# Attention with a compressive memory in front of a gated layer: the memory term as 64 more keys of the half score blocks

## The chip, the core and the metric

The kernel runs on one core of one Trainium2 chip. The metric is device time in microseconds, the median of several runs; the time before is 565.52 us.

## What is computed

A batch of 4 with 8 heads, 576 positions and a head width of 64, all in float32. Each head adds two things, weighted with a gate g per head: causal softmax attention, and a retrieval from a memory matrix M with a normaliser z.

```python
scores = scale * np.matmul(q, k.transpose(0, 1, 3, 2))
scores = np.where(causal, -1000000000.0, scores)
scores = scores - scores.max(-1, keepdims=True)
a = np.exp(scores)
a /= a.sum(-1, keepdims=True) + 1e-09
local = np.matmul(a, v)
def phi(x):
    return np.where(x > 0, x, np.exp(x) - 1.0) + 1.0
q_p = phi(q)
mem_ret = np.einsum('bhsd,bhde->bhse', q_p, M_prev)
mem_norm = np.einsum('bhsd,bhd->bhs', q_p, z_prev)[..., None] + 1e-06
g = 1.0 / (1.0 + np.exp(-beta))[None, :, None, None]
out = g * (mem_ret / mem_norm) + (1 - g) * local
```

The 2304 positions x 512 columns of `out` then go through a gated layer: `((x @ w1) * (x @ w2)) @ w3 @ w_out`, 512 to 1024 to 1024 to 512.

## The kernel before

**Pairs.** The work goes by pairs of heads: 16 of them, 0 to 15, four to a batch. A pair's q and k lie transposed in one tile `raw`, head a of the two in partitions 64a to 64a + 63. Queries are cut into a first chunk of 64 and four of 128 (chunks c = 0 to 4); chunk c sees KE[c] = 64, 192, 320, 448, 576 keys. So a chunk has c full key blocks of 128 and one half block of 64.

**A pair on the engines.** TensorE makes the scores of both heads (s_all, L205; chunk 0 of both heads in one product with the block-diagonal tile `qd`, s_mm0, L191). VectorE reduces them with the mask into the tiles sm (s_red, L182). ScalarE takes the exponential (s_exp, L215). VectorE normalises (s_norm, L224; the sums also carry 1 - g). TensorE transposes each 128x128 block (t_mm, L234, and L255 for chunk 0), with the half blocks filled up by 64 columns of zeros, and ScalarE copies the blocks into `pt` (L265). Then TensorE multiplies `pt` with the values v, head by head into two halves of the columns of one bank pair x (pv_mm, L281). `fin` splits x into a high and a low part, `xs` (L292 on ScalarE, L293 on VectorE).

**The memory term** comes from q in its untransposed layout, `qn`. mem_a: ScalarE, the negative part's exponential (L138, L139). mem_b: VectorE adds (L144), GpSimd multiplies with z (L146). mem_c: VectorE sums (L151), and three small operations make g over the norm (L152, L153, L157); GpSimd multiplies the features with it (L159). mem_t: TensorE transposes the features in five blocks (L165), ScalarE copies them to `mt` (L167). mem_mm: TensorE multiplies `mt` with a block-diagonal tile of the memory matrices, `md` (L271, L272), into the same x that pv_mm then adds to.

**The gated layer** runs between these steps as fill. In batch 0 the fill is w3 @ w_out (L427), with the unpacking of all weights (ScalarE L314, VectorE L318, L319; for the gate weights also L326, L327). From batch 1 on it is the gated layer of the batch before: gemm1 (L477, 12 products per half, evicted by ScalarE L483 and VectorE L486, split by ScalarE L488 and GpSimd L489) and gemm2 (L497, copied out by VectorE L502). A table, ORDER, gives the order of steps in a pair; each F in it is a slot of fill, 13 per pair. The framework's scheduler then sets the final order on each engine: it puts steps earlier or later by its own priorities where data allow.

**Loads** all go through SyncE's queue, in order: raw (L109), chunk 0's q into `qd` (L113), v (L119), qn (L124), z (L127), per batch the memory matrices (L133), the weights (L303, L388). An issue waits there until its target is free.

Of the kernel before, what the change touches and what calls it, by code (L numbers as in the profile page):

```python
# [8 lines left out]
F32 = mybir.dt.float32  # L9
# [4 lines left out]
ALU = mybir.AluOpType  # L14
# [7 lines left out]
    "lv mt t1 c c F "  # L22
# [3 lines left out]
    "t4b t5 F "  # L26
    "mm pv ma F "
    "fin F "
    "F "
    "ss mb F "  # L30
# [12 lines left out]
def attention_moe_kernel(  # L43
# [22 lines left out]
    PT = 1920  # L66
# [10 lines left out]
    z_p = pool("z")  # L77
# [16 lines left out]
    sm = [[None] + [const.tile([128, KE[c] + 64], F32, name=f"sm{a}{c}") for c in range(1, 5)] for a in range(2)]  # L94
    qd = const.tile([128, 128], F32, name="qd")
    md = const.tile([128, NC, 128], F32, name="md")
# [4 lines left out]
    raw_t, v_t, qn_t, z_t, mt_t, pt_t, sums_t, stat = ({} for _ in range(8))  # L101
# [4 lines left out]
    def load_qk(p):  # L106
        b, h = heads(p)
        t = raw_t[p] = qk_p.tile([128, 2, S], F32, tag="raw", name="raw")
        nc.sync.dma_start(out=t, in_=qkt[b, h:h + 2].rearrange("h d t s -> (h d) t s"))  # L109
        if p == 0:  # L110
            load_raw(1)
        for a in range(2):
            nc.sync.dma_start(out=qd[64 * a:64 * a + 64, 64 * a:64 * a + 64], in_=qkt[b, h + a][:, 0, 0:64])  # L113

    def load_v(p):
        b, h = heads(p)
        t = v_t[p] = v_p.tile([128, 2, 5, D], F32, tag="v", name="v")
        for a in range(2):
            nc.sync.dma_start(out=t[:, a], in_=v[b, h + a])  # L119

    def load_qn(p):
        b, h = heads(p)
        t = mem_p.tile([128, 5, 2, D], F32, tag="qn", name="qn")
        nc.sync.dma_start(out=t, in_=qn[b, h // 2])  # L124
        zt = z_p.tile([128, 2, D], F32, tag="z", name="z")
        zs = z_prev[b, h:h + 2]
        nc.sync.dma_start(out=zt, in_=bass.AP(tensor=zs.tensor, offset=zs.offset, ap=[[0, 128], [D, 2], [1, D]]))  # L127
        qn_t[p], z_t[p] = t, zt

    def load_m(b):  # L130
        src = m_prev[b].rearrange("d (j t) e -> d t j e", t=2)
        for a in range(2):
            nc.sync.dma_start(out=md[64 * a:64 * a + 64, :, 64 * a:64 * a + 64], in_=src[:, a])  # L133
# [14 lines left out]
    def mem_c(p):  # L148
        t, e = qn_t[p], stat.pop(("e", p))
        n = st_p.tile([128, 10, 1], F32, tag="n", name="n")  # L150
        nc.vector.tensor_reduce(out=n, in_=e.rearrange("p t h d -> p (t h) d"), axis=AX.X, op=ALU.add)  # L151
        nc.vector.tensor_scalar(out=n, in0=n, scalar1=1e-6, scalar2=None, op0=ALU.add)  # L152
        nc.vector.reciprocal(out=n, in_=n)  # L153
        h0 = 2 * p % H
        n3 = n.rearrange("p (t h) o -> p t (h o)", h=2)
        gb = g_sb[:, h0:h0 + 2].rearrange("p (o h) -> p o h", o=1).to_broadcast([128, 5, 2])
        nc.vector.tensor_tensor(out=n3, in0=n3, in1=gb, op=ALU.mult)  # L157
        tv = t.rearrange("p t h d -> p (t h) d")
        nc.gpsimd.tensor_tensor(out=tv, in0=tv, in1=n.to_broadcast([128, 10, D]), op=ALU.mult)  # L159

    def mem_t(p):
        t = qn_t.pop(p)
        x = ps_x.tile([128, 1024], F32, tag="x", name="x")
        for i in range(5):
            nc.tensor.transpose(x[:, 384 + 128 * i:512 + 128 * i], t[:, i].rearrange("p h d -> p (h d)"), ident)  # L165
        mt = mt_t[p] = mem_p.tile([128, S], F32, tag="mt", name="mt")
        nc.scalar.activation(out=mt, in_=x[:, 384:960], func=ACTF.Copy)  # L167
# [63 lines left out]
    def t_mm(p, what):  # L231
# [3 lines left out]
        if what in ("4a", "4b", "3a", "3b"):  # L235
            c, a = int(what[0]), "ab".index(what[1])
            for kc in range(4):
                tr(128 * kc, c, a, kc)
            s = 128 if c == 4 else 0
            d = pt[:, a, s:s + 1792].rearrange("p (k q) -> p k q", q=448)[:, :, 320:448]  # L240
            jobs = [(ps.rearrange("p (k q) -> p k q", q=128), d)]
        elif what in ("2", "1"):
            c = int(what)
            for a in range(2):
                for kc in range(2):
                    tr(256 * a + 128 * kc, c, a, kc)
            q = 128 * c - 64
            jobs = [(
                ps.rearrange("p (a k q) -> p a k q", a=2, q=128),
                pt[:, :, 0:896].rearrange("p a (k q) -> p a k q", q=448)[:, :, :, q:q + 128],  # L250
            )]
        elif what == "h":
            for a in range(2):
                tr(128 * a, 2, a, 2)
            nc.tensor.transpose(ps[:, 256:384], sm0, ident)  # L255
            jobs = [
                (ps[:, 0:256].rearrange("p (a q) -> p a q", a=2)[:, :, 64:128], pt[:, :, 1152:1216]),
                (ps[:, 256:384].rearrange("p (a q) -> p a q", a=2), pt[:, :, 0:64]),
            ]
        else:  # L260
            for a in range(2):
                tr(128 * a, 4, a, 4)
            jobs = [(ps[:, 0:256].rearrange("p (a q) -> p a q", a=2)[:, :, 64:128], pt[:, :, 1024:1088])]
        for s, d in jobs:
            nc.scalar.activation(out=d, in_=s, func=ACTF.Copy)  # L265

    def mem_mm(p):
        x = stat["x", p] = ps_x.tile([128, 1024], F32, tag="x", name="x")
        mt = mt_t.pop(p)
        lhsT = md[:, p % NC]  # L270
        nc.tensor.matmul(x[:, 384:512], lhsT=lhsT, rhs=mt[:, 0:128], start=True, stop=False)  # L271
        nc.tensor.matmul(x[:, 512:960], lhsT=lhsT, rhs=mt[:, 128:576], start=True, stop=False)  # L272

    def pv_mm(p):
        x, pt, vv = stat["x", p], pt_t.pop(p), v_t.pop(p)
        for kc in range(5):
            off = 1024 if kc == 4 else 576 * kc
            for q0, q1 in ((0, 128), (128, 576)) if kc == 0 else ((128 * kc, 576),):
                for a in range(2):
                    o = off + q0 - 128 * kc  # L280
                    nc.tensor.matmul(  # L281
                        x[64 * a:64 * a + 64, 384 + q0:384 + q1], lhsT=vv[:, a, kc], rhs=pt[:, a, o:o + q1 - q0],
                        start=False, stop=(q0 == 0 or kc == 4),
                    )
# [3 lines left out]
    def fin(p):  # L288
        x = stat.pop(("x", p))[:, 384:960]
# [257 lines left out]
    def pair_step(p, F):  # L547
        nx = p + 1 < NP
        ops = dict(
            mt=(1, lambda: mem_t(p)),  # L550
# [9 lines left out]
            t5=(1, lambda: t_mm(p, "5")),  # L560
# [11 lines left out]
            mm=(1, lambda: mem_mm(p)),  # L572
# [3 lines left out]
            mb=(nx, lambda: mem_b(p + 1)),  # L576
            mc=(nx, lambda: mem_c(p + 1)),
# [21 lines left out]
    nc.gpsimd.memset(md, 0.0)  # L599
    for a in range(2):  # L600
        nc.vector.memset(qd[64 * a:64 * a + 64, 64 - 64 * a:128 - 64 * a], 0.0)
    for c in range(1, 5):
        for a in range(2):
            nc.vector.memset(sm[a][c][:, KE[c]:KE[c] + 64], 0.0)
    nc.vector.memset(sm0[:, 64:128], 0.0)
# [5 lines left out]
    s_all(0)  # L611
    s_mm0(0)
# [37 lines left out]
    for b in range(B):  # L650
        load_m(b)
# [41 lines left out]
```

## Time and profile before

| | |
|---|---|
| median of 3 runs | 565.52 us (565.14 to 566.21) |
| profiled execution, first to last instruction | 564.3 us |
| TensorE busy | 542.7 us, 96% |
| VectorE busy | 281.2 us, 50% |
| ScalarE busy | 276.7 us, 49% |
| GpSimd busy | 106.7 us, 19% |

The profile is of one execution of its own, and of its time only the span is given; the median of the runs stands 1.2 us above it. Busy shares are averages over the whole span: batch 0, with the weights' unpacking, has other limits than what follows.

### The profile page before, as it was taken

What the parts mean: (1) busy time and instruction counts of PE and PEld (TensorE: products, weight loads), DVE (VectorE), ACT (ScalarE), POOL (GpSimd) and SP (SyncE); (2) the same over time, 40 slices, a digit from 0 to 9 for tenths busy, and PEclk for the clock granted to TensorE, in tenths of its full rate; (3) what the DMA queues carried; (4) which work ended last, traced back from release to release, by engine and by line L of the source; (5) the groups of instructions that cost most, each with busy time, mean ns of one, the idle gap of its engine ahead of it and who ended that gap; (6) DMA issues with size and microseconds to landing.
All of it is one profiled execution on the core that took longest, in us unless ns stands there. A gap on an engine that the chain in (4) does not pass through costs nothing.

```text
span 564.3 us, 9257 instructions
## 1 busy us (share of the span) xinstructions
PE 542.7 (96%) x3440; PEld 433.6 (77%) x3440; DVE 281.2 (50%) x896; ACT 276.7 (49%) x723; POOL 106.7 (19%) x137
## 2 busy tenths in 40 slices
PE   4899989799999999999999999999999999999997
PEld 2344544458896979787978898798969797998995
DVE  6986899759653436263626272624534351111110
ACT  5656775749562637173725464354625361220210
POOL 1101202010430122212230313031301220220210
PEclk9899999999999999999999999999999999999999
DMA  7991646612111202121213021311112000000001
GB/s 294 417 375 51 218 132 224 208 49 94 40 62 44 87 28 69 57 88 30 67 29 106 28 55 35 100 48 39 58 43 88 23 2 20 20 1 37 1 1 56
DMA packets 23068, 48.31 MB, mean 86 GB/s; under 512 B 6896, under 2 KB 13040, under 8 KB 21488
## 3 DMA queue, kind: packets, MB, share of 16 engines
q1 hardware_dynamic: 23024, 47.72, 25.1%
q8 instruction: 27, 0.44, 0.3%
q14 instruction: 17, 0.14, 0.1%
HBM read 43.00 MB, written 4.72 MB: 85 GB/s over the span
## 4 chain that ended last, share of the span: by engine, by line
PE 83%; DVE 8%; ACT 4%; DMA 3%; issue 1%; SPq 0%; POOL 0%; DVEq 0%; ACTq 0%; POOLq 0%
PE m L477 37%; PE m L497 18%; PE s L234 8%; PE x L281 7%; PE s L205 5%; PE m L427 3%; DMA wst<-w 2%; PE x L272 2%; PE sx L205 2%; PE x L165 1%; ACT sm L215 1%; DMA wst<-w_out 1%; DVE sm L224 1%; DVE wsp L327 1%; ACT pt L265 1%; DVE w3s L319 1%
## 5 line engine op out<-in xcount | busy, mean ns | idle before, releaser
L477 PE MATMUL m<-xs,wsp 128*128 128x288 f32 x1536 | 223.5, 299 | 0.0
L477 PEld LDWEIGHTS m<-xs,wsp 128*128 128x128 f32 x1536 | 206.9, 188 | 1.2
L489 POOL TENSOR_TENSOR ht<-a,ht 128x288 fp32r<-128x288 f32 (+2 forms) x96 | 59.0, 628 | 261.6 <-ACT ht L488 242.3
L215 ACT ACTIVATE sm<-sm,mx 128x320 f32<-128x320 f32 (+3 forms) x144 | 82.6, 575 | 45.2 <-DVE mx L182 45.1
L497 PE MATMUL m<-wH,ht 128*128 128x512 f32 x288 | 95.4, 398 | 0.0
L265 ACT ACTIVATE pt<-s 128x512 f32<-128x512 f32 (+1 forms) x144 | 63.8, 497 | 27.7 <-PE s L234 27.4
L486 DVE SCALAR_TENSOR_TENSOR a<-m,a 128x288 f32<-128x288 f32 x64 | 29.2, 456 | 91.7 <-PE m L477 87.4
L427 PE MATMUL m<-wo,w3s 128*128 128x512 f32 x128 | 63.5, 625 | 5.7 <-DVE w3s L319 3.8
L234 PE MATMUL s<-ident,sm 128*128 128x128 f32 x448 | 61.7, 273 | 3.1 <-DVE sm L224 2.9
L497 PEld LDWEIGHTS m<-wH,ht 128*128 128x128 f32 x288 | 54.1, 188 | 11.5
L234 PEld LDWEIGHTS s<-ident,sm 128*128 128x128 f32 x448 | 52.3, 140 | 10.8 <-DVE sm L224 4.5
L488 ACT ACTIVATE ht<-a 128x288 fp32r<-128x288 f32 (+2 forms) x96 | 31.4, 361 | 56.0 <-DVE a L486 56.0
L182 DVE CUSTOM_DVE_ANT_0 sm<-s,mask 128x320 f32<-128x320 f32 (+3 forms) x112 | 45.7, 448 | 23.1 <-PE s L205 23.1
L497 PE MATMUL m<-wL,ht 128*128 128x512 f32 x144 | 56.2, 390 | 0.0
L224 DVE TENSOR_SCALAR sm<-sm,sums 128x320 f32<-128x320 f32 (+3 forms) x144 | 54.2, 430 | 1.1
L146 POOL TENSOR_TENSOR e<-qn,z 128x640 f32<-128x640 f32 x16 | 25.8, 1612 | 149.0 <-DVE qn L144 149.0
L483 ACT ACTIVATE a<-m 128x288 f32<-128x288 f32 x64 | 26.3, 411 | 47.7 <-PE m L477 42.2
L281 PEld LDWEIGHTS x<-pt,v 128*64 128x64 f32 x384 | 25.0, 137 | 29.9 <-issue 23.3
L281 PE MATMUL x<-pt,v 128*64 128x448 f32 (+4 forms) x384 | 46.7, 392 | 0.0
L293 DVE TENSOR_TENSOR xs<-x,xs 128x576 fp32r<-128x576 f32 x16 | 12.1, 755 | 66.0 <-ACT xs L292 66.0
L427 PEld LDWEIGHTS m<-wo,w3s 128*128 128x128 f32 x128 | 22.8, 197 | 28.1 <-issue 16.6
L205 PE MATMUL s<-raw 64*128 64x320 f32 (+3 forms) x256 | 38.1, 412 | 4.4 <-DMA raw<-qkt 4.4
(65 smaller groups left out, 458.0 us busy)
## 6 DMA issues: line engine op xcount, KB each, us to landing
raw<-qkt SPq DMA_DIRECT2D x16, 576.0 KB, 3.8
wst<-w3t SPq DMA_DIRECT2D x8, 1024.0 KB, 9.0
wst<-w SPq DMA_DIRECT2D x16, 512.0 KB, 4.7
qn<-qn SPq DMA_DIRECT2D x16, 320.0 KB, 3.0
v<-v SPq DMA_DIRECT2D x32, 160.0 KB, 2.3
out<-o SPq DMA_DIRECT2D x18, 256.0 KB, 2.0
wst<-w_out SPq DMA_DIRECT2D x4, 1024.0 KB, 12.1
z<-z_prev SPq DMA_DIRECT2D x16, 64.0 KB, 2.8
```

The costliest lines, as they stand in the source:

```text
L182: nc.vector.tensor_tensor_reduce(out=sm[a][c][:, lo:hi] if c else sm0[:, 0:64], in0=x, in1=mask[:, S - KE[c] + lo:S - KE[c] + hi] if c els ...
L205: nc.tensor.matmul(y, lhsT=t[r, 0, 128 * c - 64:128 * c + 64], rhs=t[r, 1, lo:hi], start=True, stop=True)
L215: nc.scalar.activation(out=x, in_=x, func=ACTF.Exp, bias=mx, scale=-1.0, accum_out=sums_of(p)[:, k:k + 1])
L224: nc.vector.tensor_scalar(out=x, in0=x, scalar1=sums_of(p)[:, k:k + 1], scalar2=None, op0=ALU.mult)
L234: tr = lambda o, c, a, kc: nc.tensor.transpose(ps[:, o:o + 128], sm[a][c][:, 128 * kc:128 * kc + 128], ident)
L265: nc.scalar.activation(out=d, in_=s, func=ACTF.Copy)
L281: nc.tensor.matmul(x[64 * a:64 * a + 64, 384 + q0:384 + q1], lhsT=vv[:, a, kc], rhs=pt[:, a, o:o + q1 - q0], start=False, stop=(q0 == 0 or ...
L427: nc.tensor.matmul(ps, lhsT=w[:, 128 * kc:128 * kc + 128], rhs=wo[:, 512 * (kc % 2):512 * (kc % 2) + 512], start=(kc == 0), stop=(kc == 7))
L477: nc.tensor.matmul(ps[:, 0:U], lhsT=w[:, i, x, j], rhs=x_t[NC * b + j][:, xx, U * u:U * u + U], start=(k == 0), stop=(k == 11))
L488: nc.scalar.activation(out=hbuf(f, 0)[:, p:p + c], in_=a[:, o:o + c], func=ACTF.Copy)
L489: nc.gpsimd.tensor_tensor(out=hbuf(f, 1)[:, p:p + c], in0=a[:, o:o + c], in1=f32(hbuf(f, 0)[:, p:p + c]), op=ALU.subtract)
L497: nc.tensor.matmul(ps, lhsT=hbuf(f, a)[:, p:p + 128], rhs=b[f], start=(k == 0), stop=(k == 23))
```

## The change

The memory term becomes 64 more keys. In every half block the 64 columns that were zeros now take the features, already multiplied with g over the norm, and the half block's values get the 64 rows of the memory matrix under their 64 rows. The transposes that the half blocks have anyway then carry the features too, and pv_mm's products with the half blocks give local plus memory. So `mt`, `md`, mem_t and mem_mm go.

The half blocks of all chunks are now products of their own, with 128 rows of contraction: per head four products over the full key blocks (512, 384, 256, 128 columns) and five over the half blocks (four of 128 columns, one of 64), where there were six over five key blocks. The value tile is split: `v` holds the four full blocks, `u` the half blocks, with the values in partitions 0 to 63 and the memory matrix in partitions 64 to 127.

The tiles sm of both heads become slices of one tile, smx, so that GpSimd can write the features of two chunks in one operation (L178), after two for chunk 0 (L175). `qn` is laid out so that the features of chunk c stand where the half block wants them, in three loads, and is double buffered like z. Chunk 0's q is copied into `qd` by GpSimd from raw (copy_qd, L120), where two loads brought it. A pair has nine loads: raw, v, u twice, the memory matrix (five copies of it in one load), qn three times, z.

```diff
 ORDER = (
-    "lv mt t1 c c F "
+    "lv t1 c c F "
     "lqn t2 th c c F "
     "t3a t3b c F "
     "t4a c F "
-    "t4b t5 F "
-    "mm pv ma F "
+    "t4b ts F "
+    "pv ma F "
     "fin F "
     "F "
-    "ss mb F "
+    "ss qd mb F "
...
+    z_p = pool("z", 2)
+    qn_p = pool("qn", 2)
...
+    def copy_qd(p):
         for a in range(2):
-            nc.sync.dma_start(out=qd[64 * a:64 * a + 64, 64 * a:64 * a + 64], in_=qkt[b, h + a][:, 0, 0:64])
+            r = slice(64 * a, 64 * a + 64)
+            nc.gpsimd.tensor_copy(out=qd[r, r], in_=raw_t[p][r, 0, 0:64])
...
+        nc.sync.dma_start(out=t, in_=y[:, :, 0:4])
         for a in range(2):
-            nc.sync.dma_start(out=t[:, a], in_=v[b, h + a])
+            nc.sync.dma_start(out=u[0:64, :, a], in_=v[b, h + a][0:64])
+        m = m_prev[b][:, h:h + 2]
+        nc.sync.dma_start(
+            out=u[64:128].rearrange("p c a d -> p c (a d)"),
+            in_=bass.AP(tensor=m.tensor, offset=m.offset, ap=[[DM, D], [0, 5], [1, 2 * D]]),
+        )
...
-        nc.sync.dma_start(out=t, in_=qn[b, h // 2])
+        t = qn_p.tile([128, 5, 2, D], F32, tag="qn", name="qn")
+        y = qn[b, h // 2]
+        nc.sync.dma_start(out=t[64:128], in_=y[0:64])
+        nc.sync.dma_start(out=t[0:64, 1:5], in_=y[64:128, 0:4])
+        nc.sync.dma_start(out=t[0:64, 0], in_=y[0:64, 0])
...
-        tv = t.rearrange("p t h d -> p (t h) d")
-        nc.gpsimd.tensor_tensor(out=tv, in0=tv, in1=n.to_broadcast([128, 10, D]), op=ALU.mult)
+        for a in range(2):
+            r = slice(64 * a, 64 * a + 64)
+            nc.gpsimd.tensor_tensor(out=sm0[r, 64:128], in0=t[r, 0, a], in1=n[r, 0, a].to_broadcast([64, D]), op=ALU.mult)
+        for k, lo, q, o in ((1, 0, 384, 192), (3, 512, 640, 576)):
+            d = smx[:, :, lo:lo + 2 * q].rearrange("p a (k q) -> p k a q", q=q)[:, :, :, o:o + D]
+            nc.gpsimd.tensor_tensor(out=d, in0=t[:, k:k + 2], in1=n[:, k:k + 2].to_broadcast([128, 2, 2, D]), op=ALU.mult)
...
-    def mem_mm(p):
-        x = stat["x", p] = ps_x.tile([128, 1024], F32, tag="x", name="x")
-        mt = mt_t.pop(p)
-        lhsT = md[:, p % NC]
-        nc.tensor.matmul(x[:, 384:512], lhsT=lhsT, rhs=mt[:, 0:128], start=True, stop=False)
-        nc.tensor.matmul(x[:, 512:960], lhsT=lhsT, rhs=mt[:, 128:576], start=True, stop=False)
-
     def pv_mm(p):
...
+        x = stat["x", p] = ps_x.tile([128, 1024], F32, tag="x", name="x")
+        pt, (vv, uu) = pt_t.pop(p), v_t.pop(p)
+        jobs = [(kc, 512 * kc, 128 * kc + 64, 576) for kc in range(4)]
+        jobs += [(4 + c, SP[c], max(128 * c - 64, 0), 128 * c + 64) for c in (1, 2, 3, 4, 0)]
+        for k, o, q0, q1 in jobs:
             for a in range(2):
...
+                nc.tensor.matmul(
+                    x[64 * a:64 * a + 64, X0 + q0:X0 + q1], lhsT=vv[:, a, k] if k < 4 else uu[:, k - 4, a], rhs=pt[:, a, o:o + q1 - q0],
+                    start=k in (0, 4), stop=k in (8, 4),
+                )
```

Lines move by a few: what was L182 is L193 in the changed kernel, L205 is L216, L224 is L235, L234 is L245, L281 is L277, L293 is L289, L477 is L473, L497 is L493, L489 is L485, L502 is L498, L144 is L158, L146 is L160, L151 is L166.

On TensorE, the product with the values and what stands around it in a pair whose fill is gemm2, before:

```order
L497 MATMUL m<-wH_119,ht 128x512
L271 MATMUL x<-mt,md 128x128
L272 MATMUL x<-mt,md 128x448
L281 MATMUL x<-pt,v 64x128 x2
L281 MATMUL x<-pt,v 64x448 x4
L281 MATMUL x<-pt,v 64x320 x2
L281 MATMUL x<-pt,v 64x192 x2
L281 MATMUL x<-pt,v 64x64 x2
```

and in the changed kernel, the same place:

```order
L493 MATMUL m<-wH_114,ht 128x512
L277 MATMUL x<-pt,v 64x512 x2
L277 MATMUL x<-pt,v 64x384 x2
L277 MATMUL x<-pt,v 64x256 x2
L277 MATMUL x<-pt,v 64x128 x2
L277 MATMUL x<-pt,u 64x128 x8
L277 MATMUL x<-pt,u 64x64 x2
```

The two products of the memory are gone, and 12 products with the values have become 18.

On VectorE, from the copy xs of one pair to the first score reductions of the next, with a gemm2 copy (o) between, before:

```order
L293 TENSOR_TENSOR xs<-x,xs 128x576
L502 COPY o<-m 128x512
L182 ISA sm_109,mx<-s,mask 128x320
L182 ISA mx 128x1
L182 ISA sm_113,mx<-s,mask 128x320
```

and in the changed kernel:

```order
L289 TENSOR_TENSOR xs<-x,xs 128x576
L158 SCALAR_TENSOR_TENSOR qn<-qn,e 128x640
L166 TENSOR_REDUCE n<-e 128x10
L167 TENSOR_SCALAR n<-n 128x10
L168 RECIPROCAL n<-n 128x10
L172 TENSOR_TENSOR n<-n,g_sb 128x10
L498 COPY o<-m 128x512
L193 ISA smx,mx<-s,mask 128x320
```

The five operations of the memory features have moved ahead of the reductions; before, they stood behind the normalisations that follow these.

On SyncE's queue, batch 0, from the qn of pair 1 to the first loads of gate weights (wst<-w), before:

```order
L124 DMA qn<-qn 128x640
L127 DMA z<-z_prev 128x128
L303 DMA wst<-w 128x1024
L113 DMA qd<-qkt 64x64 x2
L119 DMA v<-v 128x320 x2
L303 DMA wst<-w 128x1024
L109 DMA raw<-qkt 128x1152
```

and in the changed kernel, from pair 1's values on:

```order
L128 DMA v<-v 128x2x256
L130 DMA u<-v 64x5x64
L113 DMA raw<-qkt 128x1152
L130 DMA u<-v 64x5x64
L132 DMA u<-m_prev 64x5x128
L141 DMA qn<-qn 64x640
L142 DMA qn<-qn 64x512
L143 DMA qn<-qn 64x128
L146 DMA z<-z_prev 128x128 x2
L141 DMA qn<-qn 64x640
L142 DMA qn<-qn 64x512
L143 DMA qn<-qn 64x128
```

The first three loads of gate weights come right behind these; before, the first stood ahead of pair 1's values and the second ahead of pair 2's raw.

## Rows read from the trace of the kernel before

**Rows 1.** The page's busy times: engine, us and share, instructions.

```profile
PE 542.7 (96%) x3440; PEld 433.6 (77%) x3440; DVE 281.2 (50%) x896; ACT 276.7 (49%) x723; POOL 106.7 (19%) x137
```

**Rows 2.** Stretches: length; busy PE, PEld, DVE, ACT, POOL; clock, DMA share, GB/s.

```profile
80.00:100.00 20.00, 17.95 (x96) 9.98 (x97) 19.12 (x44) 11.80 (x24) 3.09 (x2) 1.00 0.58 193
...
258.00:288.00 30.00, 30.00 (x225) 26.94 (x225) 14.07 (x49) 16.88 (x49) 8.46 (x15) 1.00 0.16 46
```

**Rows 3.** The chain that ended last, in order: start us, us, what.

```profile
108.56 1.32 PE s L234 x10
...
114.54 0.22 PE x L271 x2
114.77 0.75 PE x L272 x2
115.52 2.85 PE x L281 x24
...
128.69 0.55 PE x L165 x5
...
132.16 1.60 PE m L477 x12
...
543.84 16.36 PE m L497 x72
```

**Rows 4.** The page's costliest groups: busy us, mean ns | idle before.

```profile
L234 PEld LDWEIGHTS s<-ident,sm 128*128 128x128 f32 x448 | 52.3, 140 | 10.8 <-DVE sm L224 4.5
...
L483 ACT ACTIVATE a<-m 128x288 f32<-128x288 f32 x64 | 26.3, 411 | 47.7 <-PE m L477 42.2
```

**Rows 5.** Timeline of VectorE, one pair's memory features: start us, us, [idle before].

```profile
281.52 0.82 DVE L144 SCALAR_TENSOR_TENSOR qn<-qn,e 128x640 f32<-128x640 f32 x1
...
284.01 0.82 DVE L151 TENSOR_REDUCE n<-e 128x10 f32<-128x640 f32 x1 [1.67 <-POOL e L146]
...
285.33 0.17 DVE L157 TENSOR_TENSOR n<-n,g_sb 128x10 f32<-128x10 f32 x1
```

**Rows 6.** Timeline of VectorE: xs to the first reductions of pairs 5 and 6.

```profile
146.00 0.75 DVE L293 TENSOR_TENSOR xs<-x,xs 128x576 fp32r<-128x576 f32 x1
...
149.63 0.49 DVE L182 CUSTOM_DVE_ANT_0 sm<-s,mask 128x320 f32<-128x320 f32 x1 [2.52 <-PE s L205]
...
175.03 0.76 DVE L293 TENSOR_TENSOR xs<-x,xs 128x576 fp32r<-128x576 f32 x1 [5.37 <-ACT xs L292]
178.66 0.69 DVE L502 COPY o<-m 128x512 f32<-128x512 f32 x1 [2.87 <-PE m L497]
...
179.72 0.49 DVE L182 CUSTOM_DVE_ANT_0 sm<-s,mask 128x320 f32<-128x320 f32 x1 [0.37 <-PE s L205]
```

**Rows 7.** Timelines: five normalisations and the first transposes, pairs 5 and 8.

```profile
156.69 1.88 DVE L224 TENSOR_SCALAR sm<-sm,sums 128x320 f32<-128x320 f32 x5
...
159.38 0.60 PE L234 MATMUL s<-ident,sm 128*128 128x128 f32 x4
...
246.48 1.29 DVE L224 TENSOR_SCALAR sm<-sm,sums 128x320 f32<-128x320 f32 x5
...
247.44 0.67 PE L234 MATMUL s<-ident,sm 128*128 128x128 f32 x4
```

**Rows 8.** GpSimd beside pair 5's normalisations, its smallest product, pair 5's chunk 0, raw's landing.

```profile
156.96 0.80 POOL L489 TENSOR_TENSOR ht<-a,ht 128x288 fp32r<-128x288 f32 x1 [2.42 <-ACT ht L488]
...
L489 POOL TENSOR_TENSOR ht<-a,ht 128x96 fp32r<-128x96 f32 x32 | 13.2, 413 | 88.2 <-ACT ht L488 88.2
...
153.01 0.33 PE L191 MATMUL s<-raw,qd 128*128 128x64 f32 x2
...
raw<-qkt SPq DMA_DIRECT2D x16, 576.0 KB, 3.8
```

**Rows 9.** Waits (us in total, times, longest) and the page's landing of gate weights.

```profile
ACT wp L314 <- DMA wst<-w: 7.5, 5, 2.7
...
wst<-w SPq DMA_DIRECT2D x16, 512.0 KB, 4.7
```

## What was predicted

> **What bounds the kernel now.** I read the page's busy times first, then the stretches, then the chain that ended last, and only then single engines. TensorE is busy for 542.7 of 564.3 us [rows 1]. The stretches show where the missing 22 us lie. From 80 to 100 us TensorE is busy for 17.95 of 20 us while VectorE has 19.12, so the first stretch, in which weights are unpacked beside the attention, belongs to VectorE and to loads. From 258 to 288 us TensorE is busy all 30 us at a granted clock of 1.00, with VectorE at 14.1, ScalarE at 16.9 and GpSimd at 8.5 [rows 2]. The chain says from when on: its first piece after the last load and normalisation is pair 3's transposes at 108.56, and from there to the last product at 543.84 every piece is TensorE's [rows 3]. So after 108.56 us every microsecond that is taken off TensorE comes off the end, unless TensorE then waits for somebody. Before it, TensorE's work is free.
>
> **What TensorE loses and gains, per pair.** Three terms, all from the chain, where a piece lasts until the next one starts.
> Removed, the five transposes of the memory features: 0.55 us [rows 3]. Pairs 4 to 15 have theirs after 108.56: 12 x 0.55 = 6.6 us.
> Removed, the product with the memory matrix: 0.22 + 0.75 = 0.97 us [rows 3], in pairs 3 to 15: 13 x 0.97 = 12.6 us.
> Added, in the product with the values: a head had 1600 columns (128 + 448 + 448 + 320 + 192 + 64) and gets 1856 (512 + 384 + 256 + 128, then 4 x 128 + 64). The two heads run side by side, since 2 x 1600 columns take 2.85 us while 448 columns over the full width take 0.75 [rows 3]. 256 more columns at 2.85/1600 are 0.46 us. At the full-width rate (0.75/448) they are 0.43; with the 0.18 us that this rate leaves of the 2.85 put down to 12 matmuls, six more of these bring it to 0.52. I take 0.46: 13 x 0.46 = 6.0 us, with 5.6 and 6.8 as ends.
> The number of score transposes stays at 29, in fewer and fuller banks. Sum on TensorE: 6.6 + 12.6 - 6.0 = **13.2 us**.
> A thing that could spoil the third term: the new pieces are only 128 columns wide, and a weight load is shown with 140 ns [rows 4]. But the transposes that need such loads follow each other every 0.11 us [rows 3]: loads run under the product before them. I put this at zero.
>
> **What the change adds to waits.** Two things, both on the way from a pair's scores to its transposes.
> First, the order on VectorE. Before, the memory features' small operations stand behind the normalisations. Now features are loaded one pair earlier, and the scheduler has put the operations of the next pair between the copy of the finished pair (xs) and the score reductions, in pairs 5 to 13. That chain is add, GpSimd's product, sum, three small ones: from 281.52 to 285.50, so 3.98 us, in which VectorE waits 1.67 us for GpSimd [rows 5]. Queued behind it are the reductions, the exponentials that wait for them, the normalisations and TensorE's transposes. What is free for it is the time from the end of xs to the first reduction. In pair 5 that is 146.75 to 149.63, or 2.88 us; in pair 6 it is 175.79 to 179.72, or 3.93, but there a copy of 0.69 us stands behind the chain as well [rows 6]. The other nine rooms are about pair 6's or wider. So the reductions come 1.1 us late in pair 5, 0.7 in pairs 6 and 10 (the same pattern), and at most 0.1 elsewhere. In pairs 5, 9 and 13 ScalarE also does an eviction of 0.4 us [rows 4] ahead of the exponential that the chain begins with: 1.5, 0.2 and 0.2.
> Second, GpSimd. The copies of chunk 0's q (two of 64x64) wait for the next raw load. It lands 3.8 us after its issue, which follows the chunk-0 product at 153.01 in pair 5 [rows 8], so near 157: right in that pair's normalisations, 156.69 to 158.57 [rows 7]. Those five take 1.88 us with a GpSimd product of 0.80 beside them and 1.29 us without one, in pair 8 [rows 7, 8]. So they stand still for 0.6 of 0.8 us. GpSimd has no copy of this kind in the trace; its smallest product, 96 columns, takes 413 ns [rows 8]. By columns that is 0.28 us at 64, and if smaller ones are no faster 0.41: I take 0.34, so 0.7 for two and 0.5 us of it on the normalisations (ends 0 and 0.8).
> The Trainium skill's page "SBUF — State Buffer", section "SBUF: two separate sides", has this as an exclusive lock: of a GpSimd operation and a VectorE operation in a two-port mode, whichever starts first keeps the shared port pair to its end and the other blocks fully. The rows of pairs 5 and 8 agree in kind. By the rule the two copies would cost their whole 0.7 us in each of the five pairs below, 1 us more in all: 557.
> What has to be used up first is the slack between the normalisation that the first transposes read and these transposes. The last 0.16 us of the five is chunk 0's, which they don't read. Pair 5: 158.41 to 159.38, or 0.97; in pair 8 the transposes begin at 247.44, while the five are still running: none [rows 7]. The transposes of the features stood in this gap, so 0.55 goes: 0.42 is left in pair 5. In pair 8 the new order has 5 more gate products ahead (14 for 9), in pair 4, which has no slack either, 12 for 6; at 0.133 us each [rows 3] that leaves 0.12 and 0.25. Pairs 9 and 13 are like pair 5, 0.4; all others keep more than comes late.
> Stalls of TensorE: pair 5, 1.5 + 0.5 - 0.42 = 1.6. Pair 4, where the add (0.82) has slipped in among the normalisations: 0.82 + 0.5 - 0.25 = 1.1. Pair 8, 0.5 - 0.1 = 0.4; pairs 9 and 13, 0.2 + 0.5 - 0.4 = 0.3 each. **3.7 us** in all. The lower end is 0 (the rooms hold), the upper twice that.
>
> **What costs nothing.** ScalarE loses a copy and an eviction, but it doesn't end the chain. The nine loads of a pair are issued behind the products of the pair before and read a whole pair later; raw's median landing is 3.8 us [rows 8], and if that cover went, each pair would pay it. GpSimd writes the products one pair ahead, after the last transposes of the running pair, with that pair's product and the next scores still ahead. The first stretch I take at zero: TensorE has spare time there, VectorE keeps its operations; GpSimd's extra 1.4 us a pair can hold VectorE up, and two weight conversions move out of it. Ends: 3 us gained, 4 lost.
>
> **Sum.** 564.3 - 13.2 + 3.7 = 554.8 us of span. The median of the runs, 565.5, is 1.2 us above this execution's span, which the change doesn't touch: 556.0, range of this case 553 to 559.
>
> **Rivals.**
> Everything hidden: no stalls, perhaps some gain in the first stretch too. 565.5 - 13.2 = 552.3, down to 549. For it: VectorE is idle half of the time after the start [rows 2]. Against: pair 5's room, 1.1 us short [rows 5, 6].
> More lost: the port costs the copies' full time and the features' chain delays the reductions by 1 us more than I have it, since GpSimd may be at another product when the chain needs it. Stalls of 7 to 10 us: 559 to 562. Against: the slacks of pairs 6, 7, 10 to 12, 14 and 15.
> Slower: the start. On SyncE's queue the first load of gate weights stood ahead of pair 1's values; now the first three stand behind loads that wait for pair 0's product, pair 1's scores and pair 1's memory products. ScalarE takes its work in order, and five waits for such loads already cost it 7.5 us [rows 9]. If in pairs 1 to 3 the exponentials stand behind one more load each, with its 4.7 us to landing [rows 9], the first stretch grows by 14 us: 556.0 + 14.1 = 570. It decides from 9.5 us on. Against: the new order on ScalarE has the first gate weights behind pair 1's evictions, where they stood ahead of them.
> The weight loads of the narrow pieces not hidden: ten steps in a pair of heads with two loads each, 0.28 us for 0.11: 13 x 1.7 = 22 us more and no stalls, 565.5 - 13.2 + 22 = 574. The transposes speak against it.
>
> **How the numbers follow.** My case 0.52, everything hidden 0.20, more lost 0.17, the start 0.05, the weight loads 0.02, and 0.04 for losses that just eat the gain. A measurement of this kernel can tell about 0.2% from no change, that is 564.4 to 566.6. Faster 0.52 + 0.20 + 0.17 = 0.89, same 0.04, slower 0.07. For 8 in 10 the range takes my case and most of the two beside it: 550 to 562.
>
> **What would show it.** Transposes and products of the memory gone; a pair's product with the values near 3.3 us in 36 pieces; after 108 us idle time of TensorE of 3 to 4 us, before the first transposes of pairs 4, 5 and 8, released by VectorE's normalisation; in pair 5 the first reduction starting not when the scores are there but behind the features' chain; GpSimd's two copies inside the normalisations, and these longer for it. If the product with the values takes well over 3.4 us, the third term is wrong; if TensorE shows no idle time there, the waits are; if the transposes of pair 3 start more than 4 us off 108.6, the start is.

## The result, and the profile after

The changed kernel takes 561.06 us (median of 4 runs, 559.78 to 561.54), the kernel before, beside it on the same chip, 565.33 (565.08 to 566.21). The ratio is 0.9914, 95% interval 0.9899 to 0.9929: faster by 0.9%, where the forecast was 1.7% (556.0). The profiled execution has a span of 559.1 us, 5.2 below that of before. Lines of the code move by some: the transposes are L245 (L234 before), the product with the values L277 (L281), the exponentials L226, the normalisations L235, the gate products L473, the features' first step on ScalarE L152.

The page: busy times, and the granted clock of TensorE (the share of its full speed) in tenths over 40 slices.

```profile
PE 531.3 (95%) x3488; PEld 429.8 (77%) x3488; DVE 277.1 (50%) x887; ACT 269.2 (48%) x691; POOL 127.2 (23%) x216
...
PEclk9799999898999999999999999999999999999999
```

TensorE is busy for 11.4 us less than in [rows 1]. The chain that ended last tells where that did not come through (start us, us, what):

```profile
108.96 1.15 PE s L245 x8
...
115.01 4.00 PE x L277 x32
119.01 0.42 SPq L128
119.53 0.56 SPq L130
120.15 0.61 SPq L130
120.81 0.61 SPq L132
121.46 1.04 SPq L142
122.54 4.09 DMA qn<-qn
126.71 0.75 ACT e L152
127.48 0.74 ACT e L153
128.21 0.52 ACT wsp L322
128.73 1.31 ACT smx L226 x4
...
130.91 0.72 DVE qn L158
...
132.16 2.38 DVE smx L235 x4
134.59 1.10 PE s L245 x8
...
175.87 3.29 PE x L277 x36
```

Before, everything from 108.56 us on was TensorE [rows 3]. Now the chain leaves TensorE at pair 3's product with the values and comes back only with pair 4's transposes at 134.59. Between the two stand five issues on SyncE's queue, the landing of a load of features (qn), the features' Relu and exponential on ScalarE, pair 4's score exponentials behind them, and VectorE. The waits of TensorE after 108 us (us in total, times, longest) say what it cost:

```profile
PE s L245 <- DVE smx L235: 4.6, 2, 3.7
PE m L473 <- ACT a L479: 0.8, 2, 0.5
```

The 3.7 us are the idle time before 134.59. A table of the starts of the products with the values (first matmul of L281, L277, in us) shows in which pairs the time was lost. held6 is an experiment below, in which TensorE hardly waits after 108 us.

| pair | 3 | 4 | 5 | 6 | 10 | 11 | 15 |
|---|---|---|---|---|---|---|---|
| before | 115.4 | 141.0 | 171.4 | 200.8 | 317.9 | 348.3 | 470.7 |
| after | 114.9 | 145.5 | 175.8 | 204.1 | 317.1 | 347.5 | 465.6 |
| held6 | 114.2 | 140.1 | 169.2 | 197.6 | 310.2 | 339.7 | 457.8 |

From pair 5 to pair 15, before takes 299.3 us, held6 288.6 and the changed kernel 289.8. So TensorE's terms are worth 1.07 us a pair. The changed kernel has them nearly everywhere, but it starts pair 5 4.4 us behind the kernel before. From pair 3 to pair 4 it lost 30.5 - 25.6 + 1.1 = 6.0 us, from 4 to 5 and from 10 to 11 about 1.0 each.

**Pair 4.** ScalarE takes its instructions in order. Its timeline (start us, us, instruction, idle before):

```profile
114.42 0.68 ACT L310 ACTIVATE wp<-wst 128x512 f32<-128x512 f32 x1 [1.36 <-DVE wp L315]
...
124.94 0.44 ACT L226 ACTIVATE smx<-smx,mx 128x192 f32<-128x192 f32 x1
...
126.71 0.74 ACT L152 ACTIVATE e<-qn 128x640 f32<-128x640 f32 x1 [1.24 <-DMA qn<-qn]
...
128.64 0.65 ACT L226 ACTIVATE smx<-smx,mx 128x448 f32<-128x448 f32 x1
...
149.89 0.74 ACT L152 ACTIVATE e<-qn 128x640 f32<-128x640 f32 x1 [2.46 <-DMA qn<-qn]
```

The Relu at 126.71 is the seventh in the program: it works on pair 6's features, while pair 4's scores are under way. With two buffers, pair 6's loads can start when pair 4's products are written. The scheduler put the Relu between the fourth and the fifth of pair 4's nine exponentials; why just there, no run shows. The first of the three loads was issued at 116.92, the other two behind the four loads of pair 4's values and memory, which wait for pair 3's product:

```profile
116.92 0.47 SPq L141 DMA_DIRECT2D qn<-qn  x1
```

GpSimd writes the products of these features into the score blocks at 174 us, but pair 4's 448-column exponentials stand behind them now: 128.64 instead of 125.83 in held6. VectorE then has the features' add (0.72 us of the chain) ahead of the normalisations, and GpSimd's product with z runs beside them (VectorE, then GpSimd):

```profile
132.08 1.93 DVE L235 TENSOR_SCALAR smx<-smx,sums 128x448 f32<-128x448 f32 x2
```

```profile
131.85 1.61 POOL L160 TENSOR_TENSOR e<-qn,z 128x640 f32<-128x640 f32 x1 [1.76 <-ACT sm L226]
```

The first of the two is done only when that product is, after 1.63 us; alone it takes 0.45. From the 448-column exponentials to the transposes it is 5.95 us, in held6 4.38 (held6: ScalarE, then TensorE):

```profile
125.83 0.65 ACT L231 ACTIVATE smx<-smx,mx 128x448 f32<-128x448 f32 x1
```

```profile
130.21 0.67 PE L250 MATMUL s<-ident,smx 128*128 128x128 f32 x4
```

Then the granted clock, in stretches of 2 us (busy PE, PEld, DVE, ACT, POOL; clock, DMA share, GB/s):

```profile
134.00:136.00 2.00, 1.41 (x12) 1.38 (x13) 2.00 (x9) 0.96 (x3) 0.11 (x1) 0.97 0.12 33
136.00:138.00 2.00, 2.00 (x10) 2.00 (x9) 2.00 (x5) 1.64 (x4) 0.81 (x2) 0.50 0.00 0
138.00:140.00 2.00, 2.00 (x14) 1.98 (x13) 2.00 (x5) 0.59 (x2) 0.00 (x0) 0.67 0.00 0
```

After the idle time the clock is at its lower level (0.50, that is 1.2 of 2.4 GHz) for some 3.4 us. The shares missing from 1.00 in the three stretches make (0.03 + 0.50 + 0.33) x 2 = 1.7 us of work lost; before, all of this ran at 1.00. The third part is pair 3's product itself, 4.00 us instead of the later 3.29: two of its evictions (ScalarE's copies into `pt`) came behind the conversion of gate weights at 114.42, which had waited 1.36 us for VectorE. 3.7 + 1.7 + 0.7 = 6.1 of the 6.0 us.

**Pair 5** has the same thing smaller: the Relu of pair 7's features at 149.89 waited 2.46 us for its load, behind it stood the eviction of a gate product, and TensorE waited 0.49 us for that (the row "PE m L473 <- ACT a L479"). That is half of what was lost: between pair 4's product and pair 5's scores the same 33 gate products take 5.66 us (148.76 to 154.42), in held6 4.55 (143.44 to 147.99), and the trace shows no idle time for the rest. **Pair 11** is another thing, VectorE's order:

```profile
326.62 0.82 DVE L166 TENSOR_REDUCE n<-e 128x10 f32<-128x640 f32 x1 [2.21 <-POOL e L160]
...
328.26 0.48 DVE L193 CUSTOM_DVE_ANT_0 smx<-s,mask 128x320 f32<-128x320 f32 x1
```

The features' sum waits 2.21 us for GpSimd, and the first reduction of scores stands behind it. These scores were begun at 325.33; in the kernel before the reductions start 1.17 us after that, here 2.93. The exponentials are late for it, and an eviction behind them. TensorE shows 0.29 us of idle time there; from pair 10 to 11 it takes 0.9 us longer than in held6.

### The profile page after: what moved, and what is told of

The parts are those of the page before. It is cut to its first block, busy times and chain, and to the rows that moved or that the text cites. A ratio compares the mean times of both kernels' runs of the same rounds, so it can differ in the third digit from the quotient of the medians.

```text
span 559.1 us, 9497 instructions
## 1 busy us (share of the span) xinstructions
PE 531.3 (95%) x3488; PEld 429.8 (77%) x3488; DVE 277.1 (50%) x887; ACT 269.2 (48%) x691; POOL 127.2 (23%) x216
## 4 chain that ended last, share of the span: by engine, by line
PE 75%; DVE 9%; ACT 5%; issue 4%; DMA 4%; POOL 2%; SPq 1%; DVEq 0%; POOLq 0%; ACTq 0%
PE m L473 34%; PE m L493 18%; PE s L245 7%; PE x L277 7%; PE s L216 4%; ACT smx L226 2%; PE m L423 2%; DMA wst<-w 2%; PE sx L216 2%; DVE smx L235 2%; DMA qn<-qn 1%; DVE smx L193 1%; DMA wst<-w_out 1%; POOL smx L178 1%; DVE wp L315 1%
## 5 line engine op out<-in xcount | busy, mean ns | idle before, releaser
L473 PE MATMUL m<-xs,wsp 128*128 128x288 f32 x1536 | 225.6, 301 | 0.8 <-ACT a L479 0.8
L473 PEld LDWEIGHTS m<-xs,wsp 128*128 128x128 f32 x1536 | 208.3, 189 | 3.7 <-ACT a L479 1.5
L485 POOL TENSOR_TENSOR ht<-a,ht 128x288 fp32r<-128x288 f32 (+2 forms) x96 | 59.0, 629 | 173.3 <-ACT ht L484 173.1
L226 ACT ACTIVATE smx<-smx,mx 128x320 f32<-128x320 f32 (+3 forms) x128 | 77.3, 605 | 40.8 <-DVE mx L193 40.5
L493 PE MATMUL m<-wH,ht 128*128 128x512 f32 x288 | 95.3, 397 | 0.0
L245 PE MATMUL s<-ident,smx 128*128 128x128 f32 x448 | 61.8, 275 | 8.9 <-DVE smx L235 5.5
L245 PEld LDWEIGHTS s<-ident,smx 128*128 128x128 f32 x448 | 52.7, 141 | 16.6 <-DVE smx L235 8.2
L493 PEld LDWEIGHTS m<-wH,ht 128*128 128x128 f32 x288 | 54.1, 188 | 11.4
L493 PE MATMUL m<-wL,ht 128*128 128x512 f32 x144 | 56.3, 391 | 0.0
L235 DVE TENSOR_SCALAR smx<-smx,sums 128x192 f32<-128x192 f32 (+3 forms) x128 | 54.2, 473 | 1.0
L423 PEld LDWEIGHTS m<-wo,w3s 128*128 128x128 f32 x128 | 24.0, 201 | 32.9 <-issue 21.3
L479 ACT ACTIVATE a<-m 128x288 f32<-128x288 f32 x64 | 26.1, 407 | 46.4 <-PE m L473 41.6
L193 DVE CUSTOM_DVE_ANT_0 smx<-s,mask 128x320 f32<-128x320 f32 (+2 forms) x96 | 42.1, 486 | 11.5 <-PE s L216 11.5
L160 POOL TENSOR_TENSOR e<-qn,z 128x640 f32<-128x640 f32 x16 | 25.8, 1613 | 93.4 <-DVE qn L158 65.8
L216 PE MATMUL s<-raw 64*128 64x320 f32 (+3 forms) x256 | 37.5, 412 | 4.6 <-DMA raw<-qkt 4.6
L289 DVE TENSOR_TENSOR xs<-x,xs 128x576 fp32r<-128x576 f32 x16 | 12.1, 755 | 59.3 <-ACT xs L288 59.3
L277 PE MATMUL x<-pt,v 128*64 128x512 f32 (+3 forms) x256 | 39.2, 439 | 0.1
L216 PEld LDWEIGHTS s<-raw 64*128 64x128 f32 x256 | 23.3, 194 | 19.7 <-issue 11.8
```

The source lines that it names most:

```text
L193: nc.vector.tensor_tensor_reduce(out=sm[a][c][:, lo:hi] if c else sm0[:, 0:64], in0=x, in1=mask[:, S - KE[c] + lo:S - KE[c] + hi] if c els ...
L216: nc.tensor.matmul(y, lhsT=t[r, 0, 128 * c - 64:128 * c + 64], rhs=t[r, 1, lo:hi], start=True, stop=True)
L226: nc.scalar.activation(out=x, in_=x, func=ACTF.Exp, bias=mx, scale=-1.0, accum_out=sums_of(p)[:, k:k + 1])
L235: nc.vector.tensor_scalar(out=x, in0=x, scalar1=sums_of(p)[:, k:k + 1], scalar2=None, op0=ALU.mult)
L245: tr = lambda o, c, a, kc: nc.tensor.transpose(ps[:, o:o + 128], sm[a][c][:, 128 * kc:128 * kc + 128], ident)
L277: nc.tensor.matmul(x[64 * a:64 * a + 64, X0 + q0:X0 + q1], lhsT=vv[:, a, k] if k < 4 else uu[:, k - 4, a], rhs=pt[:, a, o:o + q1 - q0], st ...
```

## Experiments

The ratios are to the kernel before, run beside each on the same chip (medians 566.5 and 566.8 us); that of the changed kernel is 0.9914.

### ma_held: the features' first step behind the exponentials

```
+        if p:
+            o = st_p.tile([128, 1], F32, tag="o", name="o")
+            nc.vector.tensor_scalar(out=o, in0=sums_of(p - 1)[:, 1:2], scalar1=0.0, scalar2=None, op0=ALU.mult)
+            nc.scalar.activation(out=e, in_=t, func=ACTF.Relu, scale=-1.0, bias=o)
+        else:
             nc.scalar.activation(out=e, in_=t, func=ACTF.Relu, scale=-1.0)
```

> Edit: the first step of the memory features of a pair (ScalarE's Relu) is made to depend on the exponentials of the pair before, by a bias of zero that VectorE makes out of their sums (one 128x1 operation a pair). Buffers, loads and all other work stay. Theory 1, the queue: in the changed kernel ScalarE takes the Relu of pair 6's features ahead of four of pair 4's nine exponentials; its loads stand on SyncE's queue behind gate weights and behind loads that wait for pair 3's product with the values, and land at 126.6 us; so TensorE idles 3.7 us before pair 4's transposes and then gets half the clock for some us, and in pair 5 the next such Relu holds up an eviction. By it this kernel has pair 4's 448-column exponentials start within 0.6 us of the reduction that they need, TensorE idle under 1 us before pair 4's transposes, a granted clock of 1.00 from 136 to 140 us, and a time of 554 us (552.5 to 555.5), 6 to 7 below the changed kernel. Theory 2, the port: GpSimd's copies and products slow VectorE; they are all still here, so 560 to 561. Theory 3, the clock falls for a reason of its own: 558.

555.66 us, ratio 0.9809 (0.9794 to 0.9824): 5.9 us below the changed kernel, by ratio. There is no idle time before pair 4's transposes, and the clock is 1.00 from 136 to 140 us. That is theory 1, and not a clock that falls by itself. The time is 0.2 us above the expected range, since the new order holds up pair 3 instead, in the first stretch. Waits and stretches of ma_held:

```profile
PE s L250 <- DVE smx L240: 3.6, 1, 3.6
```

```profile
108.00:110.00 2.00, 0.00 (x0) 0.00 (x0) 2.00 (x9) 1.34 (x4) 0.56 (x2) 0.90 0.07 22
110.00:112.00 2.00, 1.94 (x9) 1.94 (x10) 2.00 (x9) 0.60 (x1) 0.00 (x0) 0.50 0.00 0
112.00:114.00 2.00, 2.00 (x15) 2.00 (x14) 1.97 (x5) 1.63 (x4) 0.00 (x0) 0.74 0.70 248
```

TensorE waits 3.6 us before pair 3's transposes, and again the clock falls. It takes (0.50 + 0.26) x 2 = 1.5 us of work; the 0.10 that is missing from 108 to 110 us fell into the idle time.

### qn_single: one buffer for the features

```
-    z_p = pool("z", 2)
-    qn_p = pool("qn", 2)
+    z_p = pool("z", 1)
+    qn_p = pool("qn", 1)
```

> Edit: the feature tile and its z tile back to one buffer each, nothing else. Theory 1, the queue: on ScalarE the Relu (now that of pair 5) still stands ahead of pair 4's larger exponentials, and the last of its three loads still behind the loads that wait for pair 3's product, so the stall before pair 4's transposes stays at 3 to 5 us: 559 to 563. Theory 3, it is the second buffer that draws the work forward and makes the stall: with it gone the stall is gone, 553 to 555.

558.73 us, ratio 0.9861 (0.9846 to 0.9876): 3 us below the changed kernel, just under the range of theory 1, with a stall of 2.4 us instead of 3 to 5, and far above the range of theory 3. The Relu (of pair 5's features now) stands in the same place. The last of its loads is still issued behind the values', but at 120.48 instead of 122.54 (SyncE's queue), so it has landed when ScalarE comes to it:

```profile
117.23 0.60 SPq L142 DMA_DIRECT2D qn<-qn  x1
...
120.48 0.85 SPq L143 DMA_DIRECT2D qn<-qn  x1
```

```profile
124.70 0.72 ACT L152 ACTIVATE e<-qn 128x640 f32<-128x640 f32 x1
...
126.10 0.61 ACT L322 ACTIVATE wsp<-wp 128x512 fp32r<-128x512 f32 x1
126.62 0.65 ACT L226 ACTIVATE smx<-smx,mx 128x448 f32<-128x448 f32 x1
```

TensorE's wait before pair 4's transposes:

```profile
PE s L245 <- DVE smx L235: 2.4, 1, 2.4
```

So the wait for the load is only a part. ScalarE's 1.24 us of idle time are gone here, and TensorE's idle time is 3.7 - 2.4 = 1.3 us shorter. The other 2.4 us come from work that was put ahead, without a wait: 1.4 us of Relu and exponential on ScalarE, the add and the delay by GpSimd's product on VectorE. And it is not the second buffer that puts the Relu among the exponentials: with one buffer it stands there too.

### lqn_first: the features' loads ahead of the values' loads

```
-    "lv t1 c c F "
-    "lqn t2 th c c F "
+    "lqn lv t1 c c F "
+    "t2 th c c F "
```

> Edit: the loads of the features are written ahead of the loads of the values in a pair's step. The order then has the three loads of pair 6's features together, ahead of those that wait for pair 3's product; but ScalarE's Relu now stands ahead of all of pair 4's exponentials, and on VectorE the features' add and sum ahead of pair 4's score reductions. Theory 1, the queue: the loads land near 121.5, so no exponential waits for them for long; what is left is the chain on VectorE, add, GpSimd's product, sum, from about 123 to 126.5 us, with the reductions behind it 3 us late: TensorE idles 2 to 4 us before pair 4's transposes, 557 to 561. If a chain ahead of the reductions costs nothing: 554.

559.40 us, ratio 0.9883 (0.9866 to 0.9901), inside the range. The three loads are issued at 117.00 to 118.16 and the Relu runs at 120.58 without a wait for them. But VectorE has the features' chain ahead of pair 4's reductions (VectorE, then TensorE):

```profile
122.17 0.83 DVE L158 SCALAR_TENSOR_TENSOR qn<-qn,e 128x640 f32<-128x640 f32 x1 [0.76 <-ACT e L153]
124.65 0.82 DVE L166 TENSOR_REDUCE n<-e 128x10 f32<-128x640 f32 x1 [1.65 <-POOL e L160]
125.39 0.48 DVE L193 CUSTOM_DVE_ANT_0 smx<-s,mask 128x320 f32<-128x320 f32 x1
```

```profile
122.64 1.89 PE L216 MATMUL s<-raw 64*128 64x320 f32 x12
...
133.06 0.67 PE L245 MATMUL s<-ident,smx 128*128 128x128 f32 x4 [1.13 <-DVE smx L235]
```

The reductions start 2.75 us after the first score product instead of 1.17: 1.6 late, not 3. TensorE idles 1.13 us for it, not 2 to 4, and the clock stays at 1.00 there. The time is in the range all the same because of a stall that was not expected, before pair 3's transposes: TensorE waits 2.2 us for normalisations, the clock is at 0.50 from 112 to 114 us, and pair 3's product starts at 116.6 us instead of 114.9. TensorE's waits after 100 us:

```profile
PE s L245 <- DVE smx L235: 3.3, 2, 2.2
```

Loads that land in time are not enough, then, when the work that they allow is put ahead of what TensorE waits for.

### qd_dma: chunk 0's q by two loads again

```
-            nc.gpsimd.tensor_copy(out=qd[r, r], in_=raw_t[p][r, 0, 0:64])
+            nc.sync.dma_start(out=qd[r, r], in_=qkt[p // NC, 2 * (p % NC) + a][:, 0, 0:64])
```

> Edit: chunk 0's q loaded by two DMAs again in place of GpSimd's two copies. Theory 2, the port: 16 pairs without two copies of 0.26 us beside the normalisations, 1 to 3 us faster than the changed kernel. Theory 1, the queue: ScalarE's order around pair 4 is the same and SyncE has two more issues a pair, so within 1 us of the changed kernel or slower by up to 2: 560.5 to 563.

561.35 us, ratio 0.9910 (0.9895 to 0.9925): the changed kernel's. From pair 5 to pair 15 it takes 289.6 us, the changed kernel 289.8. In these pairs GpSimd's copies cost nothing that can be measured, and theory 2 falls for them. For the pairs before, this run can't tell, since the stall in pair 4 has changed too. The Relu stands in the same place and waits longer for its load (SyncE has two more issues a pair); TensorE's wait before pair 4's transposes:

```profile
PE s L245 <- DVE smx L235: 4.9, 1, 4.9
```

### held6 and held5: hold only the steps that stood in the way

```
-        if p:
+        if p >= 6:
```

(on top of ma_held; 5 in held5)

> Edit: as in ma_held, but only from pair 6's features on. The order on all engines is then that of the changed kernel up to pair 3's product, and the first Relu that moves is the very one that stood ahead of pair 4's exponentials. Theory 1, the queue: pair 3's product with the values starts near 115.0 us as in the changed kernel (ma_held 116.5), pair 4's stall is gone, so another 1 to 1.5 us below ma_held, ratio to the kernel before 0.977 to 0.980. Against it, the gain of ma_held came from the order of the pairs before: ratio 0.985 or more. If TensorE's clock in 132 to 140 us falls without the idle time ahead of it, the clock is a cause of its own; by theory 1 it stays at 1.00.

> Edit: as held6, but from pair 5's features on, so that one more Relu, with loads that land at 108 us, leaves pair 3's evictions. Theory 1, the queue: the same as held6 within 0.7 us, ratio to the kernel before 0.976 to 0.981; pair 3's product may start up to 0.7 us earlier.

held6 takes 553.32 us, ratio 0.9767 (0.9753 to 0.9782), just below the range; held5 554.13, 0.9778 (0.9763 to 0.9792). Both beat both kernels. held6 is 13.2 us faster than before (566.8 x 0.0233) and 8.3 faster than the changed kernel by ratio, with pair 3's product at 114.2 us. In held5 that product starts at 116.1, later and not earlier as expected, since TensorE waits 2.2 us for normalisations before pair 3's transposes; the time is the same within 0.7 us all the same. All the waits of TensorE after 108 us in held6, and its stretch from 136 us:

```profile
PE s L250 <- DVE smx L240: 0.2, 1, 0.2
PE m L478 <- ACT a L484: 0.2, 1, 0.2
```

```profile
136.00:138.00 2.00, 1.84 (x15) 1.61 (x14) 1.77 (x4) 2.00 (x6) 0.64 (x1) 1.00 0.68 217
```

One dependency, from pair 6 on, gives back what the changed kernel lost in pair 4 (idle time and clock), in pair 5 and in pair 11 (pairs 10 to 11: 29.5 us instead of 30.4). The order up to pair 3's product is the changed kernel's, so the gain of ma_held did not come from there. What stays is pair 3's long product, 4.3 us.

### qd_product: the two copies as products

```
-            nc.gpsimd.tensor_copy(out=qd[r, r], in_=raw_t[p][r, 0, 0:64])
+            nc.gpsimd.tensor_tensor(out=qd[r, r], in0=raw_t[p][r, 0, 0:64], in1=one[r].to_broadcast([64, 64]), op=ALU.mult)
```

> Edit: GpSimd's two copies of chunk 0's q become two 64x64 products with a tile of ones; the order on every engine is that of the changed kernel. In the changed kernel a normalisation beside such a copy is 0.00 to 0.04 us longer than one that stands alone. Theory A, what holds VectorE up is a GpSimd operation with two inputs: normalisations beside these products are 0.2 to 0.5 us longer, as beside the other products (448 columns 0.71 for 0.45). Theory B, it is the size or the 64 partitions: they stay as they are beside the copies. The time says little, since the slack in these pairs takes it: 0 to 1.5 us more than the changed kernel, ratio 0.990 to 0.994.

561.11 us, ratio 0.9904 (0.9871 to 0.9937), the same time. What counts is how long one normalisation of L235 lasts, by what GpSimd does meanwhile (mean us and number, after 108 us; each kernel's own):

```
columns   alone        beside a copy   beside a 64x64 product   beside one of 128 partitions
          (changed)    (changed)       (qd_product)             (changed; L160, L485)
320       0.380 x16    0.382 x9        0.408 x13                -
192       0.311 x14    0.322 x12       0.365 x12                -
64        0.241 x9     0.277 x3        0.333 x3                 -
448       0.448 x18    -               -                        0.713 x7
576       0.517 x11    -               0.540 x4 (changed)       0.732 x10
```

The products last 0.29 us each (minimum, median, longest in ns):

```profile
L121 POOL TENSOR_TENSOR qd<-raw,one x32: 285/292/707, 4.7 to 424.8; 64x64 f32<-64x64 f32 x32
```

Neither theory holds as it was put: a small product costs a normalisation 0.02 to 0.09 us, more than a copy (0.00 to 0.04), but far from the 0.2 expected, and from the 0.2 to 1.2 us that products over 128 partitions cost. Whether it is the number of partitions or the length wasn't tried.

## Why the prediction came out as it did

The sign and the range held; the forecast was 5 us too low, and the case "more lost" had the time right (559 to 562) with another mechanism than the one it named. The forecast's own case, 553 to 559, missed, and the wide range held in part by luck. So is it luck that the idle time predicted, 3.7 us in all, is what pair 4 shows alone: it was spread over five pairs, with 1.1 us in pair 4.

**TensorE's terms: right.** The product with the values lasts 3.29 us in 36 matmuls instead of 2.85 in 24 [rows 3], 0.44 more where 0.46 was taken. The three terms together were 0.55 + 0.97 - 0.46 = 1.06 us a pair, and held6 shows 1.07. The narrow pieces' weight loads are hidden. The sum of 13.2 us is what held6 gains, and "everything hidden" (552.3 of 565.5, a ratio of 0.977) is held6's ratio of 0.9767. That the two agree to a tenth is in part chance: by the spans held6 gains 12.9 us (551.4 for 564.3), with 1.0 lost in pair 3's long product and 0.8 gained at the start and the end.

**The first stretch at zero: right within its ends.** Pair 3's transposes start at 108.96, 0.4 us later than before. The rival of the slower start did not come. GpSimd's extra work, for which the text took 1.4 us a pair without a row, is 1.3 (127.2 instead of 106.7 us over 16 pairs).

**The copies on GpSimd (term b, 0.5 us in five pairs): wrong in size.** Two copies last 0.55 us (estimate 0.7), and in pair 5 they fell where they were expected, in the normalisations:

```profile
162.73 1.13 DVE L235 TENSOR_SCALAR smx<-smx,sums 128x320 f32<-128x320 f32 x4
163.78 0.29 DVE L235 TENSOR_SCALAR sm<-sm,sums 128x64 f32<-128x64 f32 x1
```

```profile
163.47 0.55 POOL L120 COPY qd<-raw 64x64 f32<-64x64 f32 x2 [2.76 <-PE m L473]
```

But these five normalisations are done in 1.34 us, where [rows 7] has 1.88 with a GpSimd product beside them and 1.29 without. By the table above, a pair's five would lose at most 0.06 us to copies. The price had been taken from a product of 0.80 us, as a share of the time, and put on a copy. The Trainium skill's page "SBUF — State Buffer", section "SBUF: two separate sides", has the other engine blocked for the whole instruction of the one that starts first, when VectorE's is in a two-port mode. The trace agrees for the products over 128 partitions (the 1.63 us above); for the 64x64 copies and products it doesn't. So the port did cost something, but by the features' product in pair 4, which the text had there only as part of a chain.

**The features' chain on VectorE (term a): right in kind, its place wrong.** The reductions are late by 0.5 us in pair 5 (predicted 1.5), 0.65 in pair 6 and 0.76 in pair 10 (0.7 both), but also by 1.25 in pair 7 and 1.76 in pair 11, where at most 0.1 was predicted: the chain's length was taken from one pair, and GpSimd's product in it starts when GpSimd is free. None of it reaches the transposes of pairs 5, 8, 9 and 13, whose 2.6 us of predicted stalls are not there. In pair 5 the rows show a reason: the GpSimd product that had slowed the normalisations now stands behind them. In pair 11 about 1 us did come through, by a road not foreseen: a gate product's eviction behind late exponentials on ScalarE.

**Pair 4 (1.1 us predicted, 6.0 measured): the step that failed.** The add among the normalisations was seen. What was missed is ScalarE. The text held that features are loaded one pair earlier and that the loads, read a whole pair later, cost nothing. The chance of a stall behind a load was looked for in the gate weights (the rival of the start) and not in the features. But the chain's first step came to stand in the middle of the exponentials that the next transposes need, and with two buffers, two pairs ahead, it waits there for the youngest load of the queue. With one buffer it stands at the same place, and 2.4 of the 3.7 us of idle time stay: the second buffer is a part of the cause, the order on ScalarE and VectorE the larger one. The new order of ScalarE has it at that place; the argument went by VectorE's order and by ScalarE's rows on gate weights alone. And a wait of TensorE was priced at its length, where the 3.7 us cost 5.4 with the clock.

So 13.2 us of TensorE's work came off, 0.4 went into the start, 6.0 into pair 4, 1.0 each into pairs 5 and 11, and 0.2 into the other pairs. That leaves 4.6, measured 5.2; half a microsecond of the rest was gained after the last product with the values (90.2 us from its end to the last instruction, from 90.6).

## What to carry to other kernels

Where a scheduler sets the order, the reader of a load can come to stand ahead of work that is needed now, and on an engine that takes its work in order it holds that work up: by its own length, with one buffer as with two (qn_single, 2.4 us of idle time), and by its wait for the load as well where a second buffer lets it run further ahead (3.7 us). After such a change, read the order on every engine that the data passes through, not only on the one that does the most, and ask of each instruction that waits for a load when its result is needed. If it is late, a false dependency on something that happens just ahead of the need (here a bias of zero) puts it back for 0.14 us of VectorE a pair.

## What the hardware showed that was not expected

- A wait of TensorE cost more than its length. After idle times of 3.68 us (changed kernel, pair 4), 3.56 (ma_held, pair 3) and 2.44 (qn_single, pair 4) the granted clock was at 0.50 for about 3.4 us, and 1.5 to 1.7 us of work were lost each time. After 4.85 us (qd_dma, pair 4) it was there for 6.8 us, 2.9 of them still idle, and 2.0 us of work were lost.
- Shorter idle times came out either way. Of all the idle times of TensorE from 60 us to the end, in the nine traces, the nine of 2.2 us and more were followed by 0.50, and of the 27 between 1.0 and 2.0 us three were: 1.67 (ma_held), 1.74 (held6) and 1.89 us (changed kernel). The 1.75 us before pair 3's transposes in the kernel before and the 1.97 us in held5 were followed by 1.00, so the length of the idle time alone doesn't tell.
- GpSimd's short operations on 64 partitions hardly hold up VectorE: 0.00 to 0.04 us for a copy of 0.24 us beside a normalisation, 0.02 to 0.09 for a product of 0.29 us (3 to 13 cases each). A product of 1.61 us over 128 partitions held one up for 1.2 us.
- The queue's place counts more than the transfer: of the three feature loads of pair 6 the first was issued at 116.92 us and the last at 122.54, with a load of gate weights and four loads of values and memory between them; it had landed 4.1 us later.
